# Sigmoid attention with a bilinear feed-forward layer: blocks of 384 and 512 tokens in place of 448, and a new dealing of weight pieces and loads

## The chip, the cores and the metric

The kernel runs on one NeuronCore of one Trainium2 chip. The metric is the device time of one execution in microseconds. Five engines work side by side: TensorE (PE in the profile), VectorE (DVE), ScalarE (ACT), GpSimd (POOL), and SyncE (SP), which here only issues DMA transfers.

## The reference

Eight sequences of 448 tokens with 12 heads of 64 columns go through a sigmoid attention; its output, as 3584 rows of 768, goes through a layer with four weights (w1 and w2 are 768 x 1024, w3 is 1024 x 1024, w_out is 1024 x 768):

```python
scores = scale * np.matmul(q, k.transpose(0, 1, 3, 2)) - np.log(S)
attn = 1.0 / (1.0 + np.exp(-scores))
x = np.matmul(attn, v)
...
a = x @ w1
b = x @ w2
h = a * b @ w3
return (h @ w_out).astype(np.float32)
```

The result is in float32. The weights come in 64-bit floating point and are decoded on the chip.

## The kernel before, in words

**Numbers in two parts.** Most products are made with float32r operands, in which a number is a high part and a low remainder (`split`, line 65: one engine copies the high part, another subtracts). A product of two split matrices takes three matmuls: high with high, high with low, low with high.

**Order of the work.** The 48 head pairs (8 sequences b of 6 pairs) are worked off one after the other. A pair has four slots, one for each chunk of 128 keys (the last has 64), in the order 0, 3, 1, 2; the slots are numbered through from 0, and pair p begins at slot 4p. In a slot, line 410 onwards, the program puts in order: `prepare` (loads and splits of coming pairs), the scores of this chunk on TensorE and their sigmoids on ScalarE, a step of weight decoding if one is due, 12 matmuls of the first products of the sequence before (`up`, line 312, the filler), and the products with v of the slot before (`attend_due`). When the last product of a pair is made, in the first slot of the next pair, `combine` (line 260) splits the pair's output into xh and xl: for every sequence six tiles of 128 x 448 each.

**Plain and split pairs.** The first nine pairs (`PLAIN`) are made with plain float32 matmuls. The later ones are split: VectorE makes qs, kh (lines 158 and 159, 66), vs and al (line 217), GpSimd the low parts kl and vs; two accumulators of "av" are added by halves (line 187), and the short chunks of both heads are handled together (`short_scores`, `short_attention`).

**First products.** `up` makes, for a sequence b of 448 tokens, a = w1 x and b = w2 x: 8 column blocks times two weights times 6 contraction tiles times 3 matmuls, 288 matmuls of 448 columns at line 320. ScalarE copies a (line 328), VectorE multiplies (line 331), SyncE writes the product g to memory (line 332). Sequence b - 1 is worked off in the slots of sequence b, the last one alone behind all attention.

**Weights.** w1 and w2 come in 16 pieces (768 words a partition), w3 in 16 pieces (512 words). A piece is loaded (line 74), ScalarE makes its magnitude (line 79), VectorE decodes it in six operations (lines 86 to 102), and two steps later a piece of w1 or w2 is split (lines 66 and 67); a piece of w3 is written back to memory. `starts` says in which slots the decoding of the 16 pieces begins, `later` the same for w3; the split is due two slots later in the first 24 slots and one slot later after them. The first `EARLY` pieces go through a pool of three buffers and are loaded two pieces ahead; the others share one buffer, and the next is loaded when the one before is decoded. `EARLY` counts the starts before slot 32 and is 12 before the change.

**Who sets the order.** Up to pair 8 the order of TensorE, SyncE, ScalarE and GpSimd is the order of the program; after it only that of TensorE and SyncE. VectorE's order, and later ScalarE's and GpSimd's, is made by the compiler's scheduler. Every engine takes its queue in order, so a DMA issue that waits on SyncE holds up all the issues behind it.

**The end.** Behind the attention come the last sequence's first products (with the decoding of w_out beside them), the product of w3 and w_out (line 494, 384 matmuls of 384 columns), and the last product (line 510, 1008 matmuls of 512 columns).

Of the kernel before, what the change touches and what calls it, by code (L numbers as in the profile page):

```python
# [11 lines left out]
F32 = mybir.dt.float32  # L12
F32R = mybir.dt.float32r
U32 = mybir.dt.uint32
AF = mybir.ActivationFunctionType
ALU = mybir.AluOpType
# [9 lines left out]
def sigmoid_attention_bilinear_ffn(  # L26
# [16 lines left out]
    nc = tc.nc  # L43
    B, H, D, S = qT.shape
    DM, DF = w1.shape[0], w1.shape[1] // 2
    NT = B * S
    P = 128
    CHUNKS = [(c, min(P, S - c)) for c in range(0, S, P)]
    NC = len(CHUNKS)
    assert 2 * D == P and CHUNKS[-1][1] == D  # L50
    NPAIR = H // 2
    NK = DM // P
    NF = DF // P
    NM = DM // 2
    scale = 1.0 / math.sqrt(D)
    PLAIN = 9

    pw = ctx.enter_context(tc.tile_pool(name="pw", bufs=4))
# [1 line left out]
    ps = ctx.enter_context(tc.tile_pool(name="ps", bufs=3, space=PSUM))  # L60
    dram = ctx.enter_context(tc.tile_pool(name="dram", bufs=1, space=bass.MemoryType.DRAM))
    w3_dram = dram.tile([NF, P, NF, P], F32, name="w3_dram")
    g_dram = dram.tile([NF, P, NT], F32, name="g_dram")

    def split(dst_hi, dst_lo, src, hi_engine, lo_engine):
        hi_engine(out=dst_hi, in_=src)  # L66
        lo_engine.tensor_tensor(out=dst_lo, in0=src, in1=dst_hi, op=ALU.subtract)  # L67
# [40 lines left out]
    pm = phase_x.enter_context(tc.tile_pool(name="pm", bufs=2, side="left"))  # L108
# [3 lines left out]
    px = (px0, px1)  # L112
# [10 lines left out]
    def load_pair(b, hp):  # L123
        heads = slice(2 * hp, 2 * hp + 2)
        if b * NPAIR + hp < PLAIN:

# [13 lines left out]
    def load_v(b, hp):  # L140
        vv = pa.tile([P, NC, 2 * D], F32, name="vv")
        cols = slice(hp * 2 * D, (hp + 1) * 2 * D)
        full = (NC - 1) * P
        nc.sync.dma_start(
            out=vv[:, :NC - 1], in_=v[b, :full, cols].rearrange("(c p) e -> p c e", p=P)
        )
        for r in range(1 if b * NPAIR + hp < PLAIN else 2):
            nc.sync.dma_start(out=vv[r * D:(r + 1) * D, NC - 1], in_=v[b, full:, cols])
        return vv

    def split_pair(plain, qq, kk):

        if plain:
            return qq, kk, None, None
        qs = pf[0].tile([P, 2, S], F32R, name="qs")
        kh = pf[0].tile([P, 2, S], F32R, name="kh")
        kl = pf[0].tile([P, 2, S], F32R, name="kl")
        nc.vector.tensor_copy(out=qs, in_=qq)
        nc.vector.tensor_tensor(out=qs[D:], in0=qq[D:], in1=qs[D:], op=ALU.subtract)
        split(kh, kl, kk, nc.vector.tensor_copy, nc.gpsimd)  # L160

        ks = pf[0].tile([P, 2, P], F32R, name="ks")
        for j in range(2):
            for i, k in ((j, kh), (1 - j, kl)):
                nc.gpsimd.tensor_copy(out=ks[:, j, i * D:(i + 1) * D], in_=k[:, j, S - D:])
        return qs, kh, kl, ks

    def split_v(plain, vv):
        if plain:
            return vv  # L170

        vs = pf[0].tile([P, NC, 2, 2, D], F32R, name="vs")
        for j in range(2):
            split(vs[:, :, j, j, :], vs[:, :, j, 1 - j, :], vv[:, :, j * D:(j + 1) * D],
                  nc.vector.tensor_copy, nc.gpsimd)
        return vs
# [5 lines left out]
    def add_halves(dst, src):  # L182

        for j in range(2):
            rows, others = slice(j * D, (j + 1) * D), slice((1 - j) * D, (2 - j) * D)
            nc.scalar.copy(out=dst[rows], in_=src[j][others])  # L186
            nc.vector.tensor_tensor(out=dst[rows], in0=src[j][rows], in1=dst[rows], op=ALU.add)  # L187
# [69 lines left out]
                    start=first and m == 0, stop=last and m == len(ops) - 1,  # L257
                )

    def combine(b, accs):  # L260
        xh = px[b % 2].tile([P, S], F32R, name="xh")
        xl = px[b % 2].tile([P, S], F32R, name="xl")
        if len(accs) == 1:
            split(xh, xl, accs[0][:, :S], nc.scalar.copy, nc.vector)
            return xh, xl
        t = pm.tile([P, S], F32, name="t", bufs=1)
        add_halves(t, [acc[:, :S] for acc in accs])
        split(xh, xl, t, nc.scalar.copy, nc.vector)
        return xh, xl

    wh, wl = {}, {}
# [21 lines left out]
    def decode_weights():  # L293

        for i, (n, at, cs, _) in enumerate(jobs):
            if i + 2 < EARLY:
                load_job(i + 2)
            for k in (i, i + 1):
                if k not in fs and k in raws:
                    fs[k] = magnitude(raws[k])  # L300
            f = decode(raws.pop(i), fs.pop(i))
            if i + 1 >= EARLY and i + 1 < len(jobs):
                load_job(i + 1)
            if n == 3:
                nc.sync.dma_start(out=w3_dram[at, :, cs], in_=f)
                yield
                continue
            yield
            split(wh[n][:, at, cs], wl[n][:, at, cs], f, nc.scalar.copy, nc.vector)
            yield  # L310

    def up(b, xs, banks):

        for fc in range(NF):
            for n in (1, 2):
                acc = ps.tile([P, 512], F32, name="up", tag=next(banks), bufs=2)
                for kc in range(NK):
                    xh, xl = xs[kc]
                    for m, (w, x) in enumerate(((wh[n], xh), (wh[n], xl), (wl[n], xh))):
                        nc.tensor.matmul(  # L320
                            acc[:, :S], w[:, fc, kc], x,
                            start=(kc == 0 and m == 0), stop=(kc == NK - 1 and m == 2),
                        )
                        if (kc, m) != (NK - 1, 2):
                            yield
                if n == 1:
                    a_sb = pm.tile([P, S], F32, name="a_sb", bufs=1)
                    nc.scalar.copy(out=a_sb, in_=acc[:, :S])
                    yield
            g = pm.tile([P, S], F32, name="g", bufs=1)  # L330
            nc.vector.tensor_tensor(out=g, in0=acc[:, :S], in1=a_sb, op=ALU.mult)  # L331
            nc.sync.dma_start(out=g_dram[fc, :, b * S:(b + 1) * S], in_=g)
            yield

    def take(stream, n):
# [7 lines left out]
    pairs = [(b, hp) for b in range(B) for hp in range(NPAIR)]  # L343

    first = NPAIR * NC
    starts = [1 + i * first // 7 for i in range(7)] + [first + 1 + 3 * i // 2 for i in range(8)] + [first + 14]
    assert len(starts) == 2 * NF
    later = [(2 * NPAIR + 2 * i) * NC + 1 for i in range(2 * NF)]
    steps = starts + [s + 2 - s // first for s in starts] + later

    EARLY = sum(s < (PLAIN - 1) * NC for s in starts)
    qks, vvs = {}, {}
    for p in range(2):
        qks[p] = load_pair(*pairs[p])
        load_job(p)
        if p == 0:
            vvs[0] = load_v(*pairs[0])
    splits, vs = {0: split_pair(0 < PLAIN, *qks.pop(0))}, {0: split_v(0 < PLAIN, vvs.pop(0))}
    weights = decode_weights()
    xs = {b: [] for b in range(B)}  # L360
    filler = iter(())
    waiting = []
    accs = {}
    pf = []

    def attend_due(slot):
        while waiting and waiting[0][0] <= slot:
            _, p, c, ops = waiting.pop(0)
            if c == 0:
                accs[p] = [  # L370
                    ps.tile([P, 512], F32, name="av", bufs=2) for _ in range(1 if p < PLAIN else 2)
                ]
            attend(c, ops, vs[p], accs[p])
            if c == NC - 2:
                b = pairs[p][0]
                xs[b].append(combine(b, accs.pop(p)))
                del vs[p]

    def prepare(p, i):

        n = p + 1
        change = n in (PLAIN, PLAIN + 1)
        if i == (2 if change else 1) and n < len(pairs):
            splits[n] = split_pair(n < PLAIN, *qks.pop(n))
        if i == 0 and change:
            qks[n] = load_pair(*pairs[n])
        if i == (0 if n < PLAIN else 1) and n < len(pairs):
            vvs[n] = load_v(*pairs[n])
        if i == NC - 1 and n < len(pairs):
            vs[n] = split_v(n < PLAIN, vvs.pop(n))  # L390
        n = p + 2
        if i == (0 if n < PLAIN else 2) and n not in (PLAIN, PLAIN + 1) and n < len(pairs):
            qks[n] = load_pair(*pairs[n])
# [6 lines left out]
    for p, (b, hp) in enumerate(pairs):  # L400
# [8 lines left out]
        for i, c in enumerate(chunks):  # L409
# [13 lines left out]
            attend_due(slot)  # L423
            slot += 1
    attend_due(slot)
    take(filler, 10 ** 6)
    take(weights, 10 ** 6)
# [16 lines left out]

    banks = itertools.cycle(("up", "av"))
    filler = up(B - 1, xs[B - 1], banks)
    for jc in range(NF):
        take(filler, 10)
        for half in range(2):
            ms = slice(half * NM, (half + 1) * NM)  # L450
            src = w_out[jc * P:(jc + 1) * P].rearrange("p (m u) -> p m u", u=2)[:, ms]
# [33 lines left out]
    for ic in range(NF):  # L485
# [3 lines left out]
        for half in range(2):  # L489
            ms = slice(half * NM, (half + 1) * NM)  # L490
            acc = ps.tile([P, 512], F32, name="up", tag=next(banks), bufs=2)
# [11 lines left out]
    for tb in range(NT // TB):  # L503
        for mc in range(DM // P):
            ms = slice(mc * P, (mc + 1) * P)
            acc = ps.tile([P, 512], F32, name="up", tag=next(banks), bufs=2)
# [42 lines left out]
```

## Time and profile before

| | us |
|---|---|
| median of 3 runs | 1098.67 (1097.2 to 1100.7) |
| the profiled execution | 1100.9 |
| its span | 1099.0 |
| TensorE busy, of the span | 1072.5 |
| VectorE busy | 717.4 |
| ScalarE busy | 564.0 |
| GpSimd busy | 196.8 |

The span is what lies between the first and the last instruction of the profiled execution. A matmul's end in the profile is modelled, and matmuls overlap, so the length of one says little of the pace; the pace is the length of a run of them divided by their number. Idle time of an engine is put down to what ended it. The chain of work that ended last is followed back from the last instruction.

### The profile page before, as it was taken

The page shows a single profiled execution, that of the slowest core. Times are in us where ns is not written, and L with a number is a line of the kernel's source. Part 1 is how long each engine was busy: PE and PEld are TensorE (multiplying, and loading weights), DVE is VectorE, ACT ScalarE, POOL GpSimd, SP SyncE. Part 2 cuts the span into 40 slices and gives each one's busy share as a digit, 9 for nine tenths or more (in the row PEclk, how much of TensorE's full clock was granted, in tenths as well). Part 3 has the DMA queues.
Part 4 walks back from the last instruction along what each step waited for, and adds up shares of the span by engine and source line. Part 5 has one row for each costly group of instructions (what it writes and reads, how often), then busy time and mean ns, then how long its engine had stood idle before and what let it go on. Part 6 is the DMA issues. An engine that isn't in the chain of part 4 may idle for free.

```text
span 1099.0 us, 14114 instructions
## 1 busy us (share of the span) xinstructions
PE 1072.5 (98%) x5076; PEld 913.8 (83%) x5076; DVE 717.4 (65%) x1073; ACT 564.0 (51%) x789; POOL 196.8 (18%) x277
## 2 busy tenths in 40 slices
PE   7999689999999999999999999999999999999998
PEld 1255579999999999899999999999999988888887
DVE  5878787878888887888888877758872122122221
ACT  5753557776677777667776677753342011011100
POOL 0002142333223332332323233300000000000000
PEclk9999899999999999999999999999999999999999
DMA  7562633544444444452543524206462031333211
GB/s 240 165 195 89 151 116 95 132 116 123 114 121 132 114 125 123 108 153 73 151 121 99 161 83 109 73 20 209 140 222 79 10 125 59 123 125 125 86 49 48
DMA packets 100693, 129.15 MB, mean 118 GB/s; under 512 B 8016, under 2 KB 82960, under 8 KB 100624
## 3 DMA queue, kind: packets, MB, share of 16 engines
q1 hardware_dynamic: 100624, 128.25, 39.8%
q8 instruction: 40, 0.66, 0.3%
q14 instruction: 29, 0.24, 0.1%
HBM read 98.34 MB, written 29.88 MB: 117 GB/s over the span
## 4 chain that ended last, share of the span: by engine, by line
PE 85%; DVE 6%; DMA 4%; ACT 2%; issue 2%; SPq 1%; POOL 0%; DVEq 0%; ACTq 0%
PE up L320 38%; PE up L510 21%; PE av L255 10%; PE sp L199 8%; PE up L494 6%; DMA raw<-w 3%; PE sp L225 1%; DVE f L94 1%; ACT f L79 1%; DVE raw L99 1%; DVE f L102 1%; PE av L248 1%; DVE w L67 1%; PE sp L196 1%; DVE raw L86 0%
## 5 line engine op out<-in xcount | busy, mean ns | idle before, releaser
L320 PE MATMUL up<-xh,w 128*128 128x448 f32 x1536 | 469.9, 369 | 1.8 <-DVE g L331 1.8
L320 PEld LDWEIGHTS up<-xh,w 128*128 128x128 f32 x1536 | 290.2, 189 | 34.8 <-issue 5.3
L320 PE MATMUL up<-xl,w 128*128 128x448 f32 x768 | 282.7, 368 | 0.0
L510 PE MATMUL up<-w 128*128 128x512 f32 x1008 | 228.7, 389 | 0.0
L510 PEld LDWEIGHTS up<-w 128*128 128x128 f32 x1008 | 189.2, 188 | 39.3
L180 ACT ACTIVATE ah<-sp,bias 128x896 fp32r<-128x896 f32 x117 | 117.5, 1004 | 114.5 <-PE sp L199 113.7
L67 POOL TENSOR_TENSOR kl<-kk,kh 128x896 fp32r<-128x896 f32 x39 | 88.5, 2268 | 417.9 <-DVE kh L66 401.9
L217 DVE TENSOR_TENSOR al<-sp,ah 128x896 fp32r<-128x896 f32 x117 | 127.3, 1088 | 48.1 <-ACT sp L180 46.7
L320 PEld LDWEIGHTS up<-xl,w 128*128 128x128 f32 x768 | 145.1, 189 | 13.0
L520 DVE COPY o_sb<-up 128x512 f32<-128x512 f32 x42 | 29.0, 690 | 161.1 <-PE up L510 161.1
L66 ACT CAST w<-graw 128x1024 fp32r<-128x1024 f32 x28 | 29.3, 1055 | 174.6 <-PE up L510 170.5
L180 ACT ACTIVATE sp<-sp,bias 128x896 f32<-128x896 f32 x117 | 113.6, 971 | 0.1
L255 PE MATMUL av<-ah,vs 128*128 128x448 f32 x312 | 102.7, 369 | 3.1 <-DVE ah L239 1.3
L199 PE MATMUL sp<-qs,kh 128*128 128x448 f32 x234 | 86.7, 370 | 4.1 <-DVE kh L66 2.4
L67 POOL TENSOR_TENSOR vs<-vv,vs 128x256 fp32r<-128x256 f32 x78 | 70.9, 919 | 99.5 <-DVE vs L66 82.4
L199 PE MATMUL sp<-qs,kl 128*128 128x448 f32 x234 | 86.8, 371 | 1.9 <-POOL kl L67 1.9
L255 PE MATMUL av<-al,vs 128*128 128x448 f32 x234 | 86.0, 368 | 2.1 <-DVE al L217 2.1
L239 DVE TENSOR_TENSOR ah<-st,ah 64x448 fp32r<-64x448 f32 x78 | 57.6, 739 | 21.0 <-ACT st L180 19.2
L255 PEld LDWEIGHTS av<-ah,vs 128*128 128x128 f32 x312 | 58.7, 188 | 10.3 <-issue 3.5
L79 ACT ACTIVATE f<-raw 128x768 f32<-128x768 f32 (+2 forms) x48 | 34.0, 708 | 61.7 <-DMA raw<-w_out 20.7
L186 ACT COPY t<-av 64x448 f32<-64x448 f32 x78 | 41.2, 528 | 33.6 <-PE av L255 32.5
L180 ACT ACTIVATE ah<-st,bias 64x448 fp32r<-64x448 f32 x78 | 52.2, 669 | 4.0 <-DVE st L187 2.1
(54 smaller groups left out, 1249.0 us busy)
## 6 DMA issues: line engine op xcount, KB each, us to landing
qq<-qT SPq DMA_DIRECT2D x78, 224.0 KB, 3.9
kk<-kT SPq DMA_DIRECT2D x78, 224.0 KB, 4.4
g_dram<-g SPq DMA_DIRECT2D x64, 224.0 KB, 2.0
graw<-g_dram SPq DMA_DIRECT2D x14, 1024.0 KB, 5.4
raw<-w SPq DMA_DIRECT2D x16, 768.0 KB, 6.5
out<-o_sb SPq DMA_DIRECT2D x42, 256.0 KB, 2.0
vv<-vL SPq DMA_DIRECT2D x48, 192.0 KB, 2.7
raw<-w3T SPq DMA_DIRECT2D x16, 512.0 KB, 4.3
```

Source lines behind the costliest of these rows:

```text
L66: hi_engine(out=dst_hi, in_=src)
L67: lo_engine.tensor_tensor(out=dst_lo, in0=src, in1=dst_hi, op=ALU.subtract)
L79: nc.scalar.activation(f, raw[..., 1].bitcast(F32), AF.Abs, scale=HW_SCALE)
L180: nc.scalar.activation(dst, src, AF.Sigmoid, bias=bias[:n], scale=scale)
L186: nc.scalar.copy(out=dst[rows], in_=src[j][others])
L199: nc.tensor.matmul(sp[:, j], k[:, j, at:at + n], qs[:, j], start=m == 0, stop=m == 1)
L217: nc.vector.tensor_tensor(out=al, in0=sp, in1=ah, op=ALU.subtract)
L239: nc.vector.tensor_tensor(out=a[others, j], in0=t[rows], in1=a[rows, j], op=ALU.subtract)
L255: nc.tensor.matmul(accs[j][:, :S], v[:, c, j].rearrange("p u d -> p (u d)"), a[:, j], start=first and m == 0, stop=last and m == len(ops) - 1,
L320: nc.tensor.matmul(acc[:, :S], w[:, fc, kc], x, start=(kc == 0 and m == 0), stop=(kc == NK - 1 and m == 2),)
L494: nc.tensor.matmul(acc[:, :NM], a[:, jc], w[:, jc, ms], start=(jc == 0 and m == 0), stop=(jc == NF - 1 and m == 2),)
L510: nc.tensor.matmul(acc[:, :TB], w[:, fc, ms], g[:, at, fc % NH], start=(fc == 0 and m == 0), stop=(fc == NF - 1 and m == 2),)
```

## The change

There are four parts.

1. **Blocks of 384 and 512 tokens.** Two sequences (896 tokens) are now two blocks of 384 and 512 tokens. `combine` of an even sequence splits its first 384 tokens into xh and xl, its last 64 (`CARRY`) into a small tile xt, and SyncE writes xt to memory (`x_dram`). `combine` of the odd sequence splits its 448 tokens into the columns behind the first 64, and SyncE loads the 64 carried ones from memory into the first columns. The matmuls of line 320 so have 384 columns for even blocks and 512 for odd ones; g goes to the matching tokens.
2. **w3's pieces** are decoded in a batch, one in every pair of sequences 2 and 4 and in four pairs of sequence 6, in which the 512-token block of the sequence before is the filler. Before, one was decoded in every second pair from pair 12 on.
3. **First pieces dealt more densely.** The 16 pieces of w1 and w2 begin at slots 1, 4, 7, 10, 13, 16, 19, 22 and 25, 26, 28, 29, 31, 32, 34, 35. Before, they began at 1, 4, 7, 11, 14, 18, 21 and 25, 26, 28, 29, 31, 32, 34, 35 and 38. `EARLY` becomes 13.
4. **v a slot later.** v of a plain pair p + 1 is loaded in slot 4p + 1 and no more in slot 4p, where its load stood ahead of the load of q and k of pair p + 2. Split pairs had their load there already.

```diff
+    CARRY = 64
+    BLOCKS = (S - CARRY, S + CARRY)
...
+    x_dram = dram.tile([NK, P, 2, CARRY], F32, name="x_dram")
...
-    def combine(b, accs):
-        xh = px[b % 2].tile([P, S], F32R, name="xh")
-        xl = px[b % 2].tile([P, S], F32R, name="xl")
+    def combine(b, kc, accs):
         if len(accs) == 1:
-            split(xh, xl, accs[0][:, :S], nc.scalar.copy, nc.vector)
-            return xh, xl
-        t = pm.tile([P, S], F32, name="t", bufs=1)
-        add_halves(t, [acc[:, :S] for acc in accs])
-        split(xh, xl, t, nc.scalar.copy, nc.vector)
+            src = accs[0][:, :S]
+        else:
+            src = pm.tile([P, S], F32, name="t", bufs=1)
+            add_halves(src, [acc[:, :S] for acc in accs])
+        second = b % 2
+        n = BLOCKS[second]
+        xh = px[second].tile([P, n], F32R, name="xh")
+        xl = px[second].tile([P, n], F32R, name="xl")
+        if second:
+            for i, x in enumerate((xh, xl)):
+                nc.sync.dma_start(out=x[:, :CARRY].bitcast(F32), in_=x_dram[kc, :, i])
+            split(xh[:, CARRY:], xl[:, CARRY:], src, nc.scalar.copy, nc.vector)
+        else:
+            split(xh, xl, src[:, :n], nc.scalar.copy, nc.vector)
+            xt = pm.tile([P, 2, CARRY], F32R, name="xt")
+            split(xt[:, 0], xt[:, 1], src[:, n:], nc.scalar.copy, nc.vector)
+            nc.sync.dma_start(out=x_dram[kc], in_=xt.bitcast(F32))
         return xh, xl
...
     def up(b, xs, banks):
 
+        n_t = BLOCKS[b % 2]
+        at_t = b // 2 * 2 * S + b % 2 * BLOCKS[0]
...
-                            acc[:, :S], w[:, fc, kc], x,
+                            acc[:, :n_t], w[:, fc, kc], x,
...
-    starts = [1 + i * first // 7 for i in range(7)] + [first + 1 + 3 * i // 2 for i in range(8)] + [first + 14]
+    starts = [1 + 3 * i for i in range(8)] + [first + 1 + 3 * i // 2 for i in range(8)]
     assert len(starts) == 2 * NF
-    later = [(2 * NPAIR + 2 * i) * NC + 1 for i in range(2 * NF)]
+    later = [p * NC + 1 for p, (b, _) in enumerate(pairs) if b > 1 and b % 2 == 0][:2 * NF]
...
-        if i == (0 if n < PLAIN else 1) and n < len(pairs):
+        if i == 1 and n < len(pairs):
             vvs[n] = load_v(*pairs[n])
```

More of the change, by code (lines that the diff above doesn't have):

```diff
@@ L326, in up @@
                 if n == 1:
-                    a_sb = pm.tile([P, S], F32, name="a_sb", bufs=1)
-                    nc.scalar.copy(out=a_sb, in_=acc[:, :S])
+                    a_sb = pm.tile([P, BLOCKS[1]], F32, name="a_sb", bufs=1)[:, :n_t]
+                    nc.scalar.copy(out=a_sb, in_=acc[:, :n_t])
                     yield
-            g = pm.tile([P, S], F32, name="g", bufs=1)
-            nc.vector.tensor_tensor(out=g, in0=acc[:, :S], in1=a_sb, op=ALU.mult)
-            nc.sync.dma_start(out=g_dram[fc, :, b * S:(b + 1) * S], in_=g)
+            g = pm.tile([P, BLOCKS[1]], F32, name="g", bufs=1)[:, :n_t]
+            nc.vector.tensor_tensor(out=g, in0=acc[:, :n_t], in1=a_sb, op=ALU.mult)
+            nc.sync.dma_start(out=g_dram[fc, :, at_t:at_t + n_t], in_=g)
             yield
@@ L374, in attend_due @@
             if c == NC - 2:
-                b = pairs[p][0]
-                xs[b].append(combine(b, accs.pop(p)))
+                b, kc = pairs[p]
+                xs[b].append(combine(b, kc, accs.pop(p)))
                 del vs[p]
```

## The prediction

> **What bounds the kernel now.** I read the page first, for the busy shares and the chain that ended last:
>
> ```profile
> PE 1072.5 (98%) x5076; PEld 913.8 (83%) x5076; DVE 717.4 (65%) x1073; ACT 564.0 (51%) x789; POOL 196.8 (18%) x277
> ...
> PE 85%; DVE 6%; DMA 4%; ACT 2%; issue 2%; SPq 1%; POOL 0%; DVEq 0%; ACTq 0%
> ```
>
> TensorE carries 85% of the chain; the 15% beside it must lie in some stage. The windows by stage show which (columns: busy us and instructions of each engine, granted clock, DMA):
>
> ```profile
> 0.00:50.00 50.00, 40.32 (x154) 10.16 (x156) 32.74 (x47) 31.15 (x38) 0.20 (x4) 0.97 0.66 204
> 50.00:100.00 50.00, 49.87 (x221) 25.29 (x220) 41.58 (x58) 27.47 (x35) 2.11 (x1) 1.00 0.53 154
> 100.00:140.00 40.00, 30.86 (x119) 22.66 (x119) 28.66 (x40) 19.26 (x26) 10.34 (x14) 0.86 0.52 133
> 140.00:200.00 60.00, 56.92 (x271) 51.38 (x270) 50.81 (x76) 40.68 (x59) 21.07 (x29) 0.98 0.40 113
> ...
> 300.00:400.00 100.00, 100.00 (x491) 91.83 (x490) 81.71 (x124) 72.20 (x105) 33.44 (x49) 1.00 0.48 131
> ```
>
> From 200 us on PE is full and only fewer PE nanoseconds can shorten anything. Before 160 us it has holes, and the granted clock falls with them (0.86 of 40 us is 5.6 us of work lost). So there are two sums to make: PE's pace, and the holes.
>
> The chain in order of time gives both the pace and the transfers that stand on the path (start, us, what):
>
> ```profile
> 19.43 7.88 DMA raw<-w
> 62.38 8.88 DMA raw<-w
> 98.65 5.13 DMA raw<-w
> 110.55 5.19 DMA raw<-w
> ...
> 159.31 2.46 PE up L320 x12
> ...
> 205.91 2.44 PE up L320 x12
> ...
> 735.68 64.44 PE up L320 x312
> 800.12 66.57 PE up L494 x384
> 866.69 228.54 PE up L510 x1008
> ```
>
> Divide by the counts. A 448-column matmul of line 320 takes 203 to 205 ns between attention steps and 206.5 ns alone; a 384-column one (line 494) takes 173.4 ns, a 512-column one (line 510) 226.7 ns. A straight line through the last two is 0.416 ns a column plus 13.5 ns, and gives 200.0 ns at 448. So 448 columns cost 3 to 6 ns more than their place on the line.
>
> The holes, from the timeline of PE (in brackets the idle time and what ended it):
>
> ```profile
> 29.23 1.48 PE L248 MATMUL av<-ap,vv 128*64 128x448 f32 x4 [3.70 <-ACT ap L180]
> ...
> 111.11 0.47 PE L320 MATMUL up<-xh,w 128*128 128x448 f32 x1 [1.82 <-DVE g L331]
> 120.41 0.47 PE L255 MATMUL av<-al,vs 128*128 128x448 f32 x1 [2.07 <-DVE al L217]
> 121.90 0.71 PE L255 MATMUL av<-ah,vs 128*128 128x448 f32 x1 [1.02 <-DVE xl L67]
> 134.15 0.44 PE L199 MATMUL sp<-qs,kh 128*128 128x448 f32 x1 [2.36 <-DVE kh L66]
> 136.46 0.74 PE L199 MATMUL sp<-qs,kl 128*128 128x448 f32 x1 [1.88 <-POOL kl L67]
> 151.90 0.44 PE L199 MATMUL sp<-qs,kh 128*128 128x448 f32 x1 [1.73 <-DVE st L187]
> 156.48 0.47 PE L255 MATMUL av<-ah,vs 128*128 128x448 f32 x1 [1.07 <-DVE ah L239]
> ```
>
> I call them A (3.7 us at 29), B (1.8), C (3.1), D (4.2) and E (2.8). With the clock lost behind them (0.03 of 50 us for A; 5.6 us for B to D; 0.02 of 60 us for E) they cost about 5, 4, 5, 7 and 4 us, some 25 in all.
>
> **Part 1, the widths.**
>
> ```profile
> L320 PE MATMUL up<-xh,w 128*128 128x448 f32 x1536 | 469.9, 369 | 1.8 <-DVE g L331 1.8
> ...
> L320 PE MATMUL up<-xl,w 128*128 128x448 f32 x768 | 282.7, 368 | 0.0
> ```
>
> There are 2304 of these, 288 a block (the 369 ns are a latency with a modelled end; the pace above is what counts). Before: seven blocks beside attention at the mean of the two rows of 12, 204.2 ns, are 411.7 us, and the last at 206.5 ns is 59.5 us: 471.2 us. After: four blocks of 384 and four of 512, 1152 x 173.4 + 1152 x 226.7 ns = 460.9 us. The gain is **10 us**, all on the path, since PE is full. With 203.3 ns everywhere it is 7.5 us, with 206.5 ns 14.9 us; if the surplus belongs to this stage and not to 448 columns, it is nothing (a rival below).
>
> The Trainium skill, "TensorE: Matmul & The Clock Gate", section "Back-to-back issue gap", speaks against the change: a warm matmul takes N/2.4 + 2.5 ns, which is linear, so that 384 + 512 cost as much as twice 448 (378.3 ns) and the gain is nil. The trace does not agree: its constant is 13.4 ns at 384 and 512 and 17 to 20 ns at 448; no run so far shows line 320 itself at another width.
>
> **Part 2, the first 60 us.** Why hole A? SyncE and ScalarE tell (both take their work in program order here):
>
> ```profile
> 17.31 0.38 SPq L144 DMA_DIRECT2D vv<-vL  x1
> ...
> 19.43 1.08 SPq L74 DMA_DIRECT2D raw<-w  x2
> ```
> ```profile
> 27.40 0.89 ACT L79 ACTIVATE f<-raw 128x768 f32<-128x768 f32 x1 [4.40 <-DMA raw<-w]
> 28.19 1.00 ACT L180 ACTIVATE ap<-sp,bias 128x896 f32<-128x896 f32 x1
> ```
>
> At slot 4p, v's load waits for the last product of the pair before; the weight piece queued behind it goes out 2.1 us after it, lands 7.9 us later, and ScalarE sits in front of its magnitude with the next sigmoid behind. Loading v a slot later lets this piece go as soon as its buffer is free, some 4 us earlier: hole A goes.
>
> But the denser dealing and the carry take it back. Eight pieces now fall into 24 slots, where seven did. One piece on VectorE, from its first operation to the next foreign one, and one slot on PE:
>
> ```profile
> 50.00 0.56 DVE L86 TENSOR_SCALAR raw<-raw 128x768 uint32<-128x768 uint32 x1 [0.57 <-ACT f L79]
> ...
> 55.39 0.64 DVE L67 TENSOR_TENSOR xl<-av,xh 128x448 fp32r<-128x448 f32 x1
> ```
> ```profile
> 47.03 1.02 PE L196 MATMUL sp<-qp 64*128 64x448 f32 x4
> ...
> 48.88 1.02 PE L196 MATMUL sp<-qp 64*128 64x448 f32 x4
> ```
>
> A piece is 5.4 us of VectorE, an xl 0.64 us, six in eight pieces: 5.9 us a piece against three slots of 1.85 us, 5.6 us. VectorE becomes the limit of this stretch. Besides, in even blocks SyncE now waits at the end of slot 4p for xt, the last step of combine. When does xt end? Before, v went out as soon as the pair's last product was done:
>
> ```profile
> 52.70 0.38 SPq L144 DMA_DIRECT2D vv<-vL  x1
> ```
>
> The xl of that pair ended at 56.0, 3.3 us later; I take 3.7 us for xt. Then follow the carry's write and v's two loads (half a microsecond each, as between 17.31 and 19.43), and the pieces dealt at slots 7, 10, 13, 19 and 22 stand behind them: they land 3.7 + 1.5 + 5.2 = 10.4 us, 5.6 slots, after slot 4p ends. Piece 5, dealt at slot 10, is there at slot 14.6, and ScalarE wants it after the sigmoid of slot 13, at 14.05. With the magnitude (0.9) and the sigmoid of slot 14 (1.0) behind it, that is ready at 15.65; PE wants it at 15.5: 0.3 us lost. Piece 6, dealt at slot 13, is there at 18.6 and wanted at 17.05; the sigmoid of slot 17 comes at 19.65 and is wanted at 18.5: 2.1 us lost. Two pieces that go out together near slot 26 land after 8.9 us instead of 5.2, and cost some 2 us more. So this stretch stays as long as it was, 5 us gone and 4 to 5 come back, bounds -4 to +5. What is bought is that the weights are one piece ahead.
>
> **Part 3, 60 to 160 us.** The last pieces share one buffer, and each link (load 5.2, magnitude 0.9, decode 5.4 us) is about 12 us: 98.65 to 110.55. VectorE stands in its queue before each link's magnitude, and what PE needs (g, al, kh) stands behind. Before, the serial loads were pieces 13, 14, 15 and the first of w3; now thirteen pieces go through the three buffers, piece 13 finds the single buffer empty, and only 14, 15 and w3's are serial. One link fewer, so D, the third, goes (-7 us); B and C remain, tied to 14 and 15; E loses perhaps 1 us. I take **-8 us**, bounds -15 to 0.
>
> **Part 4, the steady pairs.** A pair is 28 attention and 48 first-product matmuls: 15.5 us before, 14.0 us in a short block, 16.6 us in a long one. VectorE is busy 81.7 of 100 us, 12.7 us a pair with half a w3 piece, whose cost I estimate from the 768-column one without its split: 4.4 x 512/768 = 3 us. Without it 11.2 us of 14.0 (80%), with a whole one and xt 14.4 of 16.6 (87%): the batches put w3 where there is room, and no engine becomes the limit. xt's two small operations lie between nothing and the 0.64 us of xl; at 0.25 us they are 2% of a pair. The 48 reads of the carry, 32 KB as these, land in about 2.3 us, and PE uses them a slot later or more: nothing.
>
> ```profile
> vv<-vL SPq DMA_DIRECT2D x87, 32.0 KB, 2.3
> ```
>
> What is thin is slack against latency:
>
> ```profile
> 318.52 1.27 DVE L187 TENSOR_TENSOR t<-av,t 64x448 f32<-64x448 f32 x2
> ...
> 320.56 0.61 DVE L67 TENSOR_TENSOR xl<-t,xh 128x448 fp32r<-128x448 f32 x1
> 320.59 0.36 PE L255 MATMUL av<-ah,vs 128*128 128x448 f32 x1
> ```
> ```profile
> DVE qs L158 <- DMA qq<-qT: 12.9, 8, 2.9
> ```
>
> The banks of av come free at 319.8 and the next product needs them at 320.6. In a short block 12 matmuls between take 0.38 us less, so 0.8 us becomes 0.4 us, and some pairs will wait. In a long block SyncE waits for xt until about 321.5, so v and the next q and k go out a microsecond or more later, and q already comes late eight times. I take **+3 us** over all pairs, bounds 0 to +10.
>
> **The sum.** Against the profiled execution (1100.9 us, span 1099.0): -10 -0 -8 +3 = -15, which gives 1086. That execution was 2.2 us above the median of the three runs, 1098.67; from the median it is **1083 us**. A difference under 0.3% (3.3 us) cannot be told from none here.
>
> **The rivals.**
> - *The surplus belongs to the stage, not to 448 columns.* The last block, alone, is slower (206.5) than the ones beside attention (203 to 205), so place does matter. Then the widths bring nothing: 1083 + 10 = 1093. Against it: both other widths show the same 13.4 ns. Chance 0.08. The linear rule of the Trainium skill, cited above, comes to the same time.
> - *Slower: SyncE's wait for the carry.* Each of the 24 pairs of even blocks puts a blocking wait in front of v, q and k. If these land later than the slack allows, VectorE stands in order before qs or vs, and al is late. It decides from 0.8 us lost a pair on: 24 x 0.8 = 19 us eats the gain; at 1 us a pair it is 1107. For it: q's eight late landings. Against it: v's products are a whole slot or two away. Chance 0.09.
> - *The holes go altogether.* If VectorE's order keeps pieces 14 and 15 from standing in the way, B, C and E go too, 12 us more: 1071. Chance 0.11.
>
> **How the numbers follow.** The forecast, 1074 to 1092, has 0.72. The other three lie on both sides; to leave out no more than 2 in 10 the range runs from 1071 to 1096. Faster by over 0.3%: 0.72 + 0.11 + half of the first rival (0.04) = 0.87; within 0.3%: its other half and the mild end of the second, 0.06; slower: 0.07.
>
> **What would show it.** Rows of 12 matmuls of line 320 at 2.08 us and 2.72 us in the chain, and the last block at 65.3 us. No wait for ap near 29 us, but short waits on ScalarE for raw before 60 us. Two holes with a lowered clock, not three, between 100 and 140 us. PE's waits for t in odd blocks, none over 0.5 us. A pace of 177 to 180 ns at 384 columns, or new waits of SyncE on xt followed by waits of VectorE on vv or qq in every even pair, would make it wrong.

## The result, and the profile after

| | us | against before |
|---|---|---|
| before, four runs | 1099.45 | |
| after, four runs | 1112.23 (1110.64 to 1112.55) | 1.0113 [1.0093, 1.0132] |
| the profiled execution of after | 1112.55, span 1110.5 | 1100.9, span 1099.0 |

The change makes the kernel 1.1% slower. The forecast was 15 us faster.

The page of after, busy shares and the chain that ended last:

```profile
PE 1074.8 (97%) x5076; PEld 901.6 (81%) x5076; DVE 713.6 (64%) x1097; ACT 564.9 (51%) x813; POOL 184.6 (17%) x277
...
PE 71%; DVE 13%; DMA 7%; SPq 3%; ACT 2%; issue 2%; POOL 1%; DVEq 0%; ACTq 0%; POOLq 0%
```

TensorE's share of the chain fell from 85% to 71%. VectorE, DMA and SyncE's queue have taken its place. The windows of after show where (columns as before: busy us of PE, PEld, DVE, ACT and POOL with their counts, granted clock, DMA share, GB/s):

```profile
0.00:50.00 50.00, 39.97 (x140) 9.87 (x140) 33.08 (x49) 29.26 (x38) 0.20 (x4) 0.90 0.71 217
50.00:100.00 50.00, 48.16 (x226) 24.04 (x224) 44.13 (x65) 29.80 (x40) 0.00 (x0) 1.00 0.57 164
100.00:140.00 40.00, 27.50 (x121) 20.85 (x117) 29.38 (x42) 17.66 (x24) 8.46 (x8) 0.86 0.47 125
140.00:200.00 60.00, 58.38 (x279) 53.22 (x280) 46.33 (x71) 41.48 (x61) 20.32 (x33) 0.95 0.37 102
200.00:300.00 100.00, 96.72 (x443) 81.48 (x441) 79.61 (x129) 63.72 (x96) 27.86 (x42) 1.00 0.47 130
300.00:400.00 100.00, 99.83 (x509) 92.85 (x510) 80.37 (x122) 74.77 (x107) 29.86 (x45) 1.00 0.46 123
```

The holes between 100 and 140 us have not shrunk (PE 27.5 us busy where it was 30.9), the first 50 us now run at a granted clock of 0.90 instead of 0.97, and there is a new hole between 200 and 300 us, where PE was to be full. The chain of after gives the pace of the new widths (start, us, what):

```profile
254.40 5.85 DMA qq<-qT
...
272.56 6.54 DMA qq<-qT
...
290.41 4.25 DMA qq<-qT
...
369.23 2.12 PE up L337 x12
...
373.00 2.75 PE up L337 x12
...
742.04 69.53 PE up L337 x312
811.58 66.57 PE up L511 x384
878.14 228.54 PE up L527 x1008
```

Twelve matmuls of 384 columns take 2.12 us, 176.7 ns each, and twelve of 512 take 2.75 us, 229.2 ns. The 312 at the end are the last 24 of 384 columns, 4.2 us, and the last block, 288 of 512: 65.3 us, as forecast. Behind line 337, lines 511 and 527 last to 0.01 us as long as before, so everything was decided ahead of 811.6 us. Three of the rows are loads of q: transfers that lay beside PE's work before now end the wait of something on the path.

Where the time went, stage by stage, can be read from the starts of the pairs' first score product on PE's timeline and from the last rows of the chain. The prediction's column adds up its own terms for each stage. The last column is e6, the version of the new blocks without the three waits that the experiments below find:

| stage | predicted | after minus before | e6 minus before |
|---|---|---|---|
| start to pair 6 (58.3 us before) | 0 | +4.7 | -0.4 |
| pair 6 to pair 12 (to 173.9) | -8.9 - 8 = -16.9 | -5.6 | -10.0 |
| pair 12 to the last 312 first products (to 735.7) | -6.5 + 3 = -3.5 | +7.3 | -2.4 |
| these 312 (to 800.1) | +5.0 | +5.1 | +5.1 |
| sum | -15.4 | +11.5 | -7.7 |

Single executions of one program differ early on: e5 and e6 below are the same program up to slot 35, and begin pair 6 at 60.63 and 57.88 us. A difference below 3 us in the first stage therefore says nothing by itself. Nearly all of it is pair 0, which takes 14.2 us in e5 and 11.3 in e6; pairs 1 to 5 take 42.4 and 42.5 us there, and 43.0 before and 47.3 in after. Where it matters, the medians decide.

### The profile page after: what moved, and what is told of

The parts are those of the page before. It is cut to its first block, busy times and chain, and to the rows that moved or that the text cites. A ratio compares the mean times of both kernels' runs of the same rounds, so it can differ in the third digit from the quotient of the medians.

```text
span 1110.5 us, 14310 instructions
## 1 busy us (share of the span) xinstructions
PE 1074.8 (97%) x5076; PEld 901.6 (81%) x5076; DVE 713.6 (64%) x1097; ACT 564.9 (51%) x813; POOL 184.6 (17%) x277
## 4 chain that ended last, share of the span: by engine, by line
PE 71%; DVE 13%; DMA 7%; SPq 3%; ACT 2%; issue 2%; POOL 1%; DVEq 0%; ACTq 0%; POOLq 0%
PE up L337 29%; PE up L527 21%; PE av L260 7%; PE sp L204 6%; PE up L511 6%; DMA qq<-qT 3%; DVE al L222 2%; DMA raw<-w 1%; DVE raw L104 1%; DMA raw<-w3T 1%; DVE f L99 1%; ACT f L84 1%; DVE t L192 1%; PE sp L230 1%; DMA vv<-vL 1%
## 5 line engine op out<-in xcount | busy, mean ns | idle before, releaser
L337 PE MATMUL up<-xh,w 128*128 128x384 f32 (+1 forms) x1536 | 465.7, 367 | 0.0
L337 PE MATMUL up<-xl,w 128*128 128x384 f32 (+1 forms) x768 | 281.9, 367 | 0.0
L72 POOL TENSOR_TENSOR kl<-kk,kh 128x896 fp32r<-128x896 f32 x39 | 83.7, 2146 | 390.4 <-DVE kh L71 331.7
L72 POOL TENSOR_TENSOR vs<-vv,vs 128x256 fp32r<-128x256 f32 x78 | 63.5, 827 | 148.8 <-DVE vs L71 148.8
L244 DVE TENSOR_TENSOR ah<-st,ah 64x448 fp32r<-64x448 f32 x78 | 52.4, 671 | 45.0 <-ACT st L185 43.7
L260 PEld LDWEIGHTS av<-ah,vs 128*128 128x128 f32 x312 | 58.6, 189 | 19.0 <-issue 11.2
```

The source lines that it names most:

```text
L244: nc.vector.tensor_tensor(out=a[others, j], in0=t[rows], in1=a[rows, j], op=ALU.subtract)
L260: nc.tensor.matmul(accs[j][:, :S], v[:, c, j].rearrange("p u d -> p (u d)"), a[:, j], start=first and m == 0, stop=last and m == len(ops) - 1,
L337: nc.tensor.matmul(acc[:, :n_t], w[:, fc, kc], x, start=(kc == 0 and m == 0), stop=(kc == NK - 1 and m == 2),)
```

## The experiments

Times are medians, ratios are to the kernel before with their 95% interval. The kernel before was run again beside each group of experiments: 1099.0 us (e1 to e4), 1098.8 (e5 to e8) and 1098.6 (e9 to e12).

**e1 and e2: the two halves of the change.** e1 takes the blocks and the carry and leaves dealing, w3 and v as they were. e2 takes those three and leaves blocks of 448.

```diff
 e1, from after:
-    starts = [1 + 3 * i for i in range(8)] + ...
+    starts = [1 + i * first // 7 for i in range(7)] + ...
-    later = [p * NC + 1 for p, (b, _) in enumerate(pairs) if b > 1 and b % 2 == 0][:2 * NF]
+    later = [(2 * NPAIR + 2 * i) * NC + 1 for i in range(2 * NF)]
-        if i == 1 and n < len(pairs):
+        if i == (0 if n < PLAIN else 1) and n < len(pairs):
```

> The blocks of 384 and 512 tokens with the carry, and the old dealing: old starts, w3's pieces in every second pair, v's load where it was. In the changed kernel the rows of twelve matmuls took 2.12 and 2.75 us, so the widths bring about 1 us. Theory C (the carry costs): SyncE's wait for xt and ScalarE's copy to xt, which waits for xl, cost some 12 us, and nothing offsets them: 1106 to 1113 us. Theory D (the dense dealing and w3's batches cost): without them the blocks alone are harmless, 1096 to 1101 us.

> The kernel before with the three other parts: dense starts, w3's pieces in batches, v a slot later; all blocks 448 and no carry. Theory C: hole A goes and one link of the serial chain with it, 5 to 12 us faster than before, 1088 to 1095 us, and no wait on SyncE takes their place. Theory D: VectorE is overfull in the first 60 us, and the batches stand in the way in sequences 2, 4 and 6 whose blocks are now 448: 1102 to 1110 us.

Measured: e1 1123.46 (1.0222 [1.0195, 1.0248]), e2 1094.68 (0.9966 [0.9952, 0.9981]). The loss is in the blocks: alone they cost 24 us. The dealing alone gains 4 us, as Theory C had it; e1 is 10 us slower than even Theory C allowed, and e10 below shows the likely larger part of the reason.

**e3 and e4: the carry's two waits.** In SyncE's waits of after (us in total, times, longest) the carry's write is third:

```profile
SPq L349 <- DVE g L348: 262.5, 47, 11.2
SPq L538 <- DVE o_sb L537: 216.3, 42, 37.0
SPq L283 <- DVE xt L72: 156.1, 24, 10.8
```

All 24 pairs of even sequences stand there, 6.5 us each. What is behind it shows in SyncE's timeline of after (start, us, instruction):

```profile
249.59 0.33 SPq L283 DMA_DIRECT2D x_dram<-xt  x1
250.00 0.39 SPq L149 DMA_DIRECT2D vv<-vL  x1
250.44 1.14 SPq L153 DMA_DIRECT2D vv<-vL  x2
251.62 0.59 SPq L79 DMA_DIRECT2D raw<-w3T  x1
252.25 1.37 SPq L320 DMA_DIRECT2D w_dram<-f  x1
253.72 1.31 SPq L140 DMA_DIRECT2D qq<-qT  x2
```

Once xt is there, the write and five issues more leave ahead of q's two. On VectorE, and then on PE, of after:

```profile
260.34 0.63 DVE L163 CAST qs<-qq 128x896 fp32r<-128x896 f32 x1 [1.22 <-DMA qq<-qT]
...
265.05 1.27 DVE L192 TENSOR_TENSOR t<-av,t 64x448 f32<-64x448 f32 x2
```
```profile
265.81 0.44 PE L260 MATMUL av<-ah,vs 128*128 128x448 f32 x1 [1.20 <-DVE t L192]
```

VectorE stands 1.2 us for q, the sums t come that much later in its queue, and PE waits 1.2 us for the bank of av that t sets free. e3 lets the write go two slots later, behind the loads of the pair:

```diff
-            nc.sync.dma_start(out=x_dram[kc], in_=xt.bitcast(F32))
+            carried.append((x_dram[kc], xt.bitcast(F32)))
...
             prepare(p, i)
+            if i == 2:
+                while carried:
+                    dst, src = carried.pop(0)
+                    nc.sync.dma_start(out=dst, in_=src)
```

The second wait is on ScalarE (timeline of after):

```profile
18.50 0.46 ACT L71 CAST xh<-av 128x384 fp32r<-128x384 f32 x1
20.95 0.21 ACT L71 CAST xt<-av 128x64 fp32r<-128x64 f32 x1 [1.98 <-DVE xl L72]
21.06 1.90 ACT L185 ACTIVATE ap<-sp,bias 64x896 f32<-64x896 f32 x2
```

The copy to xt needs only the accumulator, yet it waits until VectorE's subtraction has read that same accumulator, and two sigmoids stand behind it; PE then waits 1.78 us for ap at 22.11. e4 puts both copies ahead of both subtractions, so that there is nothing to wait for:

```diff
-            split(xh, xl, src[:, :n], nc.scalar.copy, nc.vector)
             xt = pm.tile([P, 2, CARRY], F32R, name="xt")
-            split(xt[:, 0], xt[:, 1], src[:, n:], nc.scalar.copy, nc.vector)
+            nc.scalar.copy(out=xh, in_=src[:, :n])
+            nc.scalar.copy(out=xt[:, 0], in_=src[:, n:])
+            nc.vector.tensor_tensor(out=xl, in0=src[:, :n], in1=xh, op=ALU.subtract)
+            nc.vector.tensor_tensor(out=xt[:, 1], in0=src[:, n:], in1=xt[:, 0], op=ALU.subtract)
```

> The changed kernel with the carry's write put two slots later in the program, behind the loads of v, of q and k and of the weight piece of those slots. Theory C: SyncE no longer waits in front of the loads, so q and k are on time in the steady pairs (5 to 6 us back) and the weight pieces come earlier in the first 60 us (2 us back): about 1104 us, with ScalarE's wait for xl still there. Theory D: no change, 1110 to 1113 us.

> The changed kernel with ScalarE's two copies (xh, xt) put ahead of VectorE's two subtractions, so that the copy to xt no longer stands behind xl. Theory C: ScalarE's waits for xl (10.6 us in six times) vanish and with them four or five of PE's waits for ap: 3 to 5 us back, 1107 to 1109 us, the rest is SyncE's. Theory D: no change, 1110 to 1113 us.

Measured: e3 1102.26 (1.0025 [1.0009, 1.0041]), 10 us less than after; e4 1112.01 (1.0113 [1.0085, 1.0142]), no change. In SyncE's waits of e3 the write costs 24.6 us in place of 156.1, and the new holes behind 200 us are gone:

```profile
SPq L433 <- DVE xt L72: 24.6, 12, 3.1
```

The loss does not come evenly. By the starts of the pairs, 9.2 of the 11.2 us between the traces of after and e3 lie in pairs 16 to 19 and 28 to 31; the other pairs from 12 on agree within 0.3 us. In e1 the write stands at the same place, 111.6 us in 23 waits, and yet its long pairs 13 to 17 and 25 to 29 all take 16.77 us, where pairs 16, 17 and 28 of after take 17.9 to 18.5. In e1 a w3 piece comes in every second pair, in after in each of these. So in the long pairs the wait cost something only where a w3 piece stands in every pair.

e4 begins pair 12 2.0 us ahead of after, and pair 42 0.3 us behind it: later waits took back what the copies had gained.

**e5: both edits.**

> The changed kernel with both: ScalarE's copies first and the carry's write two slots later. The late write alone took 10 us off the changed kernel, the copies alone nothing. Theory S (SyncE's wait is the carry's whole price): the same as with the late write alone, 1100 to 1103 us. Theory Q (the copies' gain of 2 us at pair 12 was real and was eaten behind it): 1098 to 1100 us.

Measured: 1097.05 (0.9987 [0.9976, 0.9997]), 5.2 us less than e3. The order of the copies is worth nothing over the whole kernel while SyncE's wait stands behind it, and five microseconds without that wait. This is Theory Q, by 1 us more than it had. The gain lies where the waits were: pairs 1 to 5 take 47.5 us in e3 and 42.4 in e5, and the granted clock over the first 50 us is 0.90 in e3 and 1.00 in e5. The two prices depend on the order in which they are taken away: -10.0 and -5.2 with the write first, -0.2 and -15.0 with the copies first.

**e6 and e7: the third serial link.** The waits of e5 still hold the hole of the prediction's link D (kh, then kl):

```profile
PE sp L204 <- DVE kh L71: 4.5, 1, 4.5
...
PE sp L204 <- POOL kl L72: 2.0, 1, 2.0
```

In after, SyncE's timeline shows what came ahead of the q and k that kh and kl are made of:

```profile
126.65 0.37 SPq L79 DMA_DIRECT2D raw<-w3T  x1
127.06 2.09 SPq L140 DMA_DIRECT2D qq<-qT  x2
```

This is w3's first piece. It takes the one buffer of the late pieces, so its issue waits until piece 15 is decoded, and q and k of pair 10 wait behind it on SyncE. e6 is e5 with that load one slot later, behind them; e7 is the same edit on e2, with blocks of 448.

```diff
-            if i + 1 >= EARLY and i + 1 < len(jobs):
+            if i + 1 >= EARLY and i + 1 < len(jobs) and i + 1 != 2 * NF:
                 load_job(i + 1)
...
             yield
+            if i + 1 == 2 * NF:
+                load_job(i + 1)
             split(wh[n][:, at, cs], wl[n][:, at, cs], f, nc.scalar.copy, nc.vector)
```

> As the run with both, and the load of w3's first piece, which waits until piece 15 is decoded, is put one slot later in the program, behind the loads of q and k of pair 10. Theory W (this load is the third link; SyncE issues q and k of pair 10 only behind it, and PE's waits for kh and kl come from that): the hole before pair 10's scores goes, 6 to 7 us with its clock, 1092 to 1096 us. Theory V (VectorE is late there anyway, whatever SyncE does): no change, 1099 to 1102 us.

> The dealing alone, all blocks 448 (1094.7 us), with w3's first load a slot later. There PE waited 1.7 us for kl and the clock fell at 121 us after a wait for al. Theory W: 2 to 4 us faster, 1090 to 1093 us. Theory V: no change, 1094 to 1096 us.

Measured: e6 1093.58 (0.9951 [0.9934, 0.9968]), 3.5 us less than e5; e7 1089.21 (0.9911 [0.9894, 0.9929]), 5.5 us less than e2. Both are faster, as Theory W had it, e6 by less than its 6 to 7 us and e7 by more than its 2 to 4. q now leaves ahead of the piece (SyncE of e6):

```profile
108.48 1.30 SPq L140 DMA_DIRECT2D qq<-qT  x2
...
120.48 0.37 SPq L79 DMA_DIRECT2D raw<-w3T  x1
```

The waits for kh and kl are gone in both; in e6 PE has waits of 1.35 us for ah at 127 us and 2.05 us for st at 143 us in their place. The hole at al stays, in e6 and in e7, behind the decoding of piece 15 (PE of e6, then of e7):

```profile
115.60 0.74 PE L260 MATMUL av<-al,vs 128*128 128x448 f32 x1 [3.90 <-DVE al L222]
```
```profile
120.65 0.74 PE L255 MATMUL av<-al,vs 128*128 128x448 f32 x1 [3.21 <-DVE al L217]
```

e7 is the fastest kernel of the study: it beats the kernel before by 0.9% and the changed one by 23 us, without the new blocks.

**e8: what the carry's own operations cost.** e6 without xt and its write; the odd blocks read zeros from memory (the lines that put them there are left out here).

```diff
-            xt = pm.tile([P, 2, CARRY], F32R, name="xt")
-            nc.scalar.copy(out=xt[:, 0], in_=src[:, n:])
-            nc.vector.tensor_tensor(out=xt[:, 1], in0=src[:, n:], in1=xt[:, 0], op=ALU.subtract)
-            carried.append((x_dram[kc], xt.bitcast(F32)))
```

> Widths without a carry to make: as the run with the later w3 load, but the even blocks split 384 tokens and drop their last 64, and the odd blocks read zeros for them (left out: the last 64 tokens of every even sequence in the first products). xt's four small operations and the carry's writes are gone, the 48 reads stay. Theory N (the widths bring next to nothing beside attention, since rows of twelve took 2.12 + 2.75 against 2 x 2.45 us): within 2 us of the run with the carry written late. Theory X (xt's operations on VectorE and ScalarE cost in the first 60 us): 3 to 6 us faster than that run.

Measured: 1093.89 (0.9952 [0.9933, 0.9970]), as e6. Once nothing waits for it, making and writing the carry is free. The 48 reads are in both kernels, so their price is not shown.

**e9: the first two blocks at 448.** Why is e7 faster than e6? e9 is e6 with the first products of sequences 0 and 1 at 448 columns, and the others at 384 and 512.

```diff
-        n_t = BLOCKS[b % 2]
+        n_t = BLOCKS[b % 2] if b > 1 else S
...
-                    xh, xl = xs[kc]
+                    xh, xl = xs[kc] if b else (other, other)
+                    xh, xl = xh[:, :n_t], xl[:, :n_t]
```

> As the run with the later w3 load (1093.6 us), but the first products of sequences 0 and 1 are made at 448 columns each, those of 2 to 7 at 384 and 512 as there. (Left out: for sequence 0 the moving operand is a piece of w1 in place of x, for sequence 1 the last 64 of its 512 columns are dropped; only the time counts.) Theory E (in the stretch of the first block PE waits for the decoding anyway, so its 8 us were never to be had, while the 512-column block behind it costs its 7 us in full): 7 us faster, 1085 to 1088 us, and faster than the dealing with all blocks at 448 (1089.2). Theory P (the widths are simply neutral, or cost 4 us spread over all blocks): 1092 to 1095 us.

Measured: 1089.52 (0.9918 [0.9890, 0.9946]), 4.1 us less than e6: four executions of 1088.2 to 1089.9 us against four of 1093.2 to 1094.4. That lies between the two theories. Both of these blocks at 448 should cost 288 x (204.2 - 176.7) = 7.9 us for the first and gain 288 x (229.2 - 204.2) = 7.2 us for the second. The second's gain is there (from pair 12 on e9 takes 7.0 us less than e6). Of the first's 8 us at most 3 are lost: e9 begins pair 12 3.1 us later than e6, and 2.1 of these are pair 0, in which the two programs are the same. So in the stretch before pair 12 the short block kept 1 to 3 of its 8 us. Against e7, e9 differs from pair 12 on only in the widths and the carry: from there to the last block e9 takes 552.4 us and e7 561.5, and the last 312 take 69.5 and 64.4 us (last rows of the chain of e6, as in e9, then of e7):

```profile
722.84 69.53 PE up L343 x312
```
```profile
725.22 64.44 PE up L322 x312
```

So where PE is full, widths gain what the pace says (three short blocks less 7.9 us each, without the 24 matmuls at the end, and two long ones more 7.2 us make -8.6; measured -9.1), and the end gives 5.1 of it back.

**e10: w3's batches.** e6 with w3 dealt as before, one piece in every second pair.

```diff
-    later = [p * NC + 1 for p, (b, _) in enumerate(pairs) if b > 1 and b % 2 == 0][:2 * NF]
+    later = [(2 * NPAIR + 2 * i) * NC + 1 for i in range(2 * NF)]
```

> As the run with the later w3 load, but w3's pieces again one in every second pair from pair 12 on, short blocks included. Theory B (a short pair has room for no piece: 11.2 + 3 us of VectorE in 14.2 us of PE): PE waits in the short pairs with a piece, 8 to 15 us slower, 1101 to 1109 us. Theory L (the pieces fit anywhere, since VectorE was only 84% busy): no change, 1092 to 1096 us.

Measured: 1107.86 (1.0090 [1.0058, 1.0121]), 14.3 us more than e6. Theory B is right. With w3 pieces beside short blocks VectorE is 85.5 of 100 us busy (70.0 of 86, or 81%, in e6) and PE is not full (windows of e10, then of e6 at the same pairs):

```profile
260.00:360.00 100.00, 95.42 (x483) 88.00 (x482) 85.51 (x123) 68.42 (x99) 30.71 (x43) 0.98 0.45 124
```
```profile
264.00:350.00 86.00, 86.00 (x455) 82.10 (x454) 69.95 (x101) 64.32 (x93) 30.25 (x43) 1.00 0.41 107
```

By the starts of the pairs, sequences 3 and 5, whose short blocks now have three pieces each, are 7.4 and 4.4 us longer than in e6, and the other sequences from pair 12 on agree within 0.3 us. By subtraction (e2 less e11 and e12 below) the batches gain only about 1 us at 448 columns. They are what makes the short blocks bearable, and by this price their lack is the larger part of e1's 24 us.

**e11 and e12: v and the dense starts alone**, each on the kernel before.

```diff
 e11:
-        if i == (0 if n < PLAIN else 1) and n < len(pairs):
+        if i == 1 and n < len(pairs):
 e12:
-    starts = [1 + i * first // 7 for i in range(7)] + [first + 1 + 3 * i // 2 for i in range(8)] + [first + 14]
+    starts = [1 + 3 * i for i in range(8)] + [first + 1 + 3 * i // 2 for i in range(8)]
```

> The kernel before with nothing but v's load a slot later. Theory A (hole A comes from the weight piece that stands behind v's wait on SyncE): the wait of 3.7 us for ap near 29 us goes, with its lowered clock, and the stretch up to slot 26 is 4 to 5 us shorter; 1094 to 1096 us. Theory R (VectorE is the limit of that stretch already): the hole moves on, less than 2 us, 1097 to 1100 us.

> The kernel before with nothing but the denser starts (and the thirteenth early piece that follows from them). Theory T (the first 60 us get VectorE-bound, and w3's first load becomes the third serial link ahead of the q and k of pair 10): hole A stays, small waits for ap come, holes B to D stay: 1099 to 1104 us. Theory G (one link fewer is a gain whatever else): 1090 to 1095 us.

Measured: e11 1093.32 (0.9953 [0.9937, 0.9968]), 5.3 us less than before; e12 1100.87 (1.0027 [1.0002, 1.0052]), 2 us more. Theory A fits e11 and Theory T fits e12. In the traces pairs 1 to 5 take 38.8 us in e11, 45.2 in e12 and 43.0 before; pair 9 of e11 is shorter by another 3.9 us, for which no cause is shown. PE's timeline shows hole A gone in e11 and there in e12:

```profile
28.69 0.97 PE L248 MATMUL av<-ap,vv 128*64 128x448 f32 x4 [0.58 <-ACT ap L180]
```
```profile
28.01 0.97 PE L248 MATMUL av<-ap,vv 128*64 128x448 f32 x4 [2.39 <-ACT ap L180]
```

## Why the prediction was wrong, point by point

**Part 1, the widths: wrong by more than half.** The step that failed is the pace: 173.4 and 226.7 ns are rows in which line 494 and line 510 run by themselves, and I put them against 204.2 ns, a row beside attention. Like with like, beside attention 384 and 512 columns take 2.12 + 2.75 = 4.87 us for 24 matmuls, and 448 columns 2 x 2.45 = 4.90: a long and a short pair together are as long as two pairs of before (16.77 + 14.24 us in e6, 2 x 15.52 before). The surplus over N/2.4 is 16.7, 17.5 and 15.9 ns at 384, 448 and 512. With four short blocks, three long ones and the last, which was priced rightly, the sum is -4 x 7.9 + 3 x 7.2 + 5.8 = -4.2 us, not -10. What is left comes of there being one more short block than long ones beside attention. "The surplus belongs to the stage", with a chance of 0.08, was the right reading of these rows; the first sign named for it, a pace of about 177 ns at 384, is what the chain shows. The linear rule cited from the Trainium skill, "TensorE: Matmul & The Clock Gate", section "Back-to-back issue gap", is right in its form for this stage, to within 1.6 ns, while its constant of 2.5 ns, which the page gives for a single isolated matmul, is not seen at any width here.

**And of these, the first block's 8 us are not on the path.** "All on the path, since PE is full" is true from 200 us on, as the prediction itself had read from the windows, but the first block is worked off in pairs 6 to 11, 58 to 174 us, the stretch with the holes. There the links of loading and decoding set the end, and shorter filler lengthens the wait behind it: e9 shows 1 to 3 of the 8 us kept. So the widths' worth was about nothing even without any new wait.

**Part 2, the first 60 us.** Hole A was read rightly: v a slot later takes it away and gains 5.3 us alone (e11). The dense starts take 2 us (e12); the prediction had them, with the carry, at 4 to 5. What it did not see is ScalarE's copy to xt. It put xt's two operations between nothing and 0.64 us, by their length; what counted was whom the copy waits for (groups of ScalarE's waits in after):

```profile
ACT xt L71 <- DVE xl L72: 10.6, 6, 3.1
```

The six are plain pairs of sequence 0, whose accumulator both engines read in PSUM; where t in SBUF is read there is no such wait. Its price is 5.2 us (e5 against e3), shown once SyncE's wait is gone. The Trainium skill, "PSUM — Partial Sum Buffer", section "Terms", says that two engines may not be on the same bank and quadrant (32 partitions) at once, two reads included; an order kept between them for that reason agrees with these rows, though no run here shows the reason itself.

**Part 3, hole D: stayed.** The prediction counted the links right (14, 15 and w3's first) but let D go with the one that was dropped. D hangs on the third serial load, which stands on SyncE right ahead of pair 10's q and k. Before, that is piece 15, and w3's first leaves only later (SyncE of before):

```profile
122.65 0.37 SPq L74 DMA_DIRECT2D raw<-w  x1
123.07 1.30 SPq L135 DMA_DIRECT2D qq<-qT  x2
...
138.40 0.37 SPq L74 DMA_DIRECT2D raw<-w3T  x1
```

In after the links move up by one place, and w3's first, now the third, stands in that place (126.65 us, above). What went in place of D are B, with no wait over 0.9 us left near 111 us, and most of E (2.8 us before, 1.1 after). So the sign named for this part, two holes with a lowered clock between 100 and 140 us, came true by luck: they are C and D, where B and C were meant. PE's timeline of after has C and D longer than before, 5.5 and 6.2 us in place of 3.1 and 4.2:

```profile
121.77 0.47 PE L260 MATMUL av<-al,vs 128*128 128x448 f32 x1 [4.47 <-DVE al L222]
123.26 0.71 PE L260 MATMUL av<-ah,vs 128*128 128x448 f32 x1 [1.02 <-DVE xl L72]
138.13 0.71 PE L204 MATMUL sp<-qs,kh 128*128 128x448 f32 x1 [4.49 <-DVE kh L71]
140.57 0.74 PE L204 MATMUL sp<-qs,kl 128*128 128x448 f32 x1 [1.73 <-POOL kl L72]
```

Moving the one load gained 3.5 and 5.5 us (e6, e7) of the 7: the size of D was of the right order, what it hangs on was not.

**Part 4, the steady pairs: the mechanism was named, the size was wrong.** That v, q and k "go out a microsecond or more later" is what the trace shows, and VectorE's wait for q there is followed by PE's wait for t: five times, 5.3 us in all, where the kernel before has one such wait of 0.5 us. VectorE waits for q no oftener than before; the late landings now reach PE. The write cost 10 us in all (e3), most of them in pairs 16 to 19 and 28 to 31, where +3 was taken for all pairs. The price lay at the upper bound of 0 to +10. The second rival, which ends slower by this very wait, was set against a gain of 19 us that was not there: without the wait (e3) the kernel is still 3 us slower than before, so no gain was left to eat. Its 24 equal pairs were not what the traces show either. What was read rightly here: xt's operations cost nothing by themselves once no engine waits at them (e8), and the w3 batches keep the engines under their limit (e10).

**The account.** From after at 1112.2 us: the write later -10.0, the copies first -5.2, w3's load later -3.5, which is e6 at 1093.6. Back to blocks of 448 is another -4.4, e7 at 1089.2. Read the other way, dealing and v with w3's load moved gain 9.6 us on the kernel before, and in no version here do the blocks pay: all eight cost 4.4 us at best, and on sequences 2 to 7 alone, e9, they end even with e7. By the stages of the table the forecast missed by 4.7, 11.3, 10.8 and 0.1 us: in the first stage mainly the copy to xt, in the second D and the short block that was not on the path, in the third the write and the pace of the widths.

**What stays open.** e9 and e7 have the same widths before pair 12, but e9 begins that pair 2.8 us later in its trace. This is pair 10, 18.3 us in e9 and 15.6 in e7: VectorE makes kh there behind t, at 140.6 us, and not ahead of it, at 136.1 us as in e7; its xl takes 2.55 us in place of 0.61, beside GpSimd's kl; and PE then waits 1.1 us for st. VectorE's order is the scheduler's, and whether the carry changed it is not shown; without this, blocks from sequence 2 on would gain the 4 us that they show behind it. Nor is it settled why 448 columns have a pace of 203 to 205 ns beside attention and 206.5 alone, while 384 and 512 are slower beside attention than alone.

## What to carry to other kernels

Price an edit with rows from the stage in which it will run, and ask of that stage alone whether the engine you relieve sets its end: a saving on TensorE in a stretch bound by a chain of loads is mostly a longer wait. For a DMA that must wait for data on a shared issue queue, the cost is not the transfer but every load behind it, so put it behind the loads that are wanted next. When several such waits stand one behind another, one edit alone may show nothing (e4); remove them together before you call one free.

## What the runs showed of the hardware

The time of a float32r matmul over N/2.4, which is the 0.416 ns a column of the prediction's line, is not one constant: 13.4 ns at 384 and 512 columns by themselves (173.4, 226.7 ns), 16 to 17.5 ns for all three widths between attention steps (176.7, 204.2, 229.2 ns), 20 ns for 448 by itself (206.5 ns). A copy of 64 columns, 0.21 us long, held up its engine's queue for up to 3.1 us, because it stood behind another engine's queued read of the same accumulator (six waits, 10.6 us, in after). And the granted clock falls after short waits: 0.90 over the first 50 us in after, where PE's longest waits behind the first 10 us are 1.8 us at 22 us and 2.5 us at 41 us.
